# Attention and experts on one core: gate columns from f16 halves of v that the DMA queue turns, one division for two heads, and attention's order by due alone

## The chip, the core and the metric

One core of a Trainium2 chip runs one program. The metric is the device time of that program in microseconds (us). A core has a matrix engine (TensorE, PE in the profile, with its weight loads as PEld), three engines for vectors and scalars (VectorE or DVE, ScalarE or ACT, GpSimd or POOL), a queue that issues transfers (SyncE or SP) and 16 DMA engines that carry them. Each engine works through its own list in order; between engines there are semaphores.

## What is computed

Causal attention with a decay, then a layer of eight experts of which each token uses one. Shapes: 8 batches, 8 heads, 576 tokens, 64 elements a head; 4608 tokens of 512 elements in all.

```python
def _attn_ref(q, k, v, f):
    scores = scale * np.matmul(q, k.transpose(0, 1, 3, 2))
    cum = np.cumsum(np.log(np.clip(f, 0.0001, 1.0)), axis=-1)
    scores = np.where(causal, -1000000000.0, scores + cum[..., :, None] - cum[..., None, :])
    attn = np.exp(scores - np.max(scores, axis=-1, keepdims=True))
    attn = attn / (np.sum(attn, axis=-1, keepdims=True) + 1e-09)
    return np.matmul(attn, v)

def _moe_ref(x, modality_id, w_gate, modality_bias, w1, w2):
    logits = x @ w_gate + modality_bias[modality_id]
    e_idx = np.argmax(logits, axis=1)
    probs = softmax(logits)
    for e in range(E):
        h = np.maximum(x[e_idx == e] @ w1[e], 0.0)
        out[e_idx == e] = probs[e_idx == e, e, None] * (h @ w2[e])
    return out
```

The expert of a token is an argmax over logits, so they are kept close to f32: a value is carried as a high half and a remainder, and a product of two values as three products of halves.

## The kernel before

**Two parts.** Attention comes first; it ends by writing every token's row to a list of its expert (`xs`). Then the experts run in tiles of 256 tokens (class `Moe`). One of its preparations (`early`) lies inside attention.

**Attention's tiles.** The work goes by pairs of heads p (32 of them, four a batch) and by batches b. A pair's steps, with the engine of each: `raw` loads k and q (SP); `hi` and `lo` split them (ScalarE, GpSimd, L372 and L378); `cum` puts the decay sums in place (SP, L383); `mm` computes rough scores for the row maxima (TensorE, L511 to L522) and `mr` reduces them (VectorE); `sp` transposes the maxima (TensorE, L543), `ssp` negates and splits them (VectorE, L549 and L550) and `so` moves them beside q (SP, L557); `s` computes the scores with decay and maximum inside (TensorE, L577 to L592); `e` takes the exponential (ScalarE, L601 and L607); `h` and `r` split it into two f16 parts Ph and Pl (ScalarE L622; GpSimd and VectorE L634); `w`, once a head, forms the weighted sum (TensorE, L660 to L662: 45 matmuls of 128x128 weights, Ph and Pl, by 73 columns); `d`, once a head, divides (VectorE, L671 to L676).

**Gate columns.** The 73 columns of a head's v are a column of ones (the softmax's sum), 64 elements of v, and 8 gate columns: the head's v times its rows of the router's weights. The weighted sum of a gate column is the head's part of the logits, so that the logits come out with attention. v is scaled by a power of two per batch (`vm`, `v1`, `v3`, `v2`: L398 to L428) and split into f16 halves `vh` and `vl` (ScalarE L481, VectorE L488), which have two buffers, for even and odd batches. The gate columns come from a second, transposed f32 copy of v: `vt` loads it for a pair of heads (SP, L457, 320 KB), `gv` scales the router's weights (ScalarE, L453), `kg` multiplies (TensorE, L462: five f32 matmuls with 16 columns, each shown as two records), `kh` and `kl` split the product into the gate columns of vh and vl (ScalarE L467, VectorE L474).

**Routing.** When a batch's heads are divided, `ga` sums the parts of the logits and `rt` picks the expert and the place in its list (VectorE, GpSimd, ScalarE, with a few small matmuls, L723 to L728); `sc` writes the rows out (GpSimd, L769).

**PSUM.** Eight banks: six are three buffers of two banks (`ps`) for `mm` and `s`; one (`po`) holds a weighted sum until it is divided; one (`pb`) is shared by all the small steps: `sp`, `v1`, `v3`, `v2`, `kg` and the router's counts. Only in the last two pairs does the second head's sum use `pb` (function `room`).

**The order.** A planner (class `Plan`) lists all steps with the engine, an estimated duration, what they come after and which buffers they take. `order` is a list scheduler: at each turn it takes the step that could start earliest by a clock of these durations, and the one with the smaller due time where two are equal. The due times are 12.0 us times the pair plus an offset by kind of step from the table `DUE`, with offsets of their own for the first two and last two pairs. The program issues the steps in that order; each engine gets its own in that order.

## Time and profile before

| | us |
|---|---|
| median of 3 runs | 864.05 |
| lowest, highest | 863.62, 870.75 |
| the profiled execution | 868.65 |
| its span, first to last instruction | 866.9 |

The busy share of an engine is an average over two parts with different limits: attention runs until about 384 us, the experts after it. A row of a view of groups has the line of the code, the engine, the operation, what it writes and reads, its shapes and count, then busy us, the mean duration of one in ns, and the idle time of the engine before it. A row of the order of time has start, duration, engine, line, operation, names, shapes and count. Records of TensorE overlap, since matmuls are pipelined: what a block takes is seen from its start to the start of the next.

### The profile page before, as it was taken

To read this page: it belongs to the slowest core of one execution; us is meant where nothing else is said; L and a number is where in the kernel's file an instruction comes from. 1 tells how busy PE (TensorE), PEld (TensorE's weight loads), DVE (VectorE), ACT (ScalarE), POOL (GpSimd) and SP (SyncE) were. 2 spreads that over 40 slices of the span, in tenths; PEclk is the share of its full clock that TensorE was granted. 3 is DMA by queue.
4 is the path that set the end of the run, shared out by engine and by line. 5 is a ranking of instruction groups with operands and counts; after the bars stand their busy time and mean duration, and the time that the engine had idled before them with its cause. 6 is when DMAs were issued, how large, how long until landed. Compare 5 with 4: busy or idle time off the path is not lost. (4 is left out here: it accounts for less than half of the span.)

```text
span 866.9 us, 23516 instructions
## 1 busy us (share of the span) xinstructions
PE 815.1 (94%) x9701; PEld 732.3 (84%) x9701; DVE 649.9 (75%) x1211; ACT 523.0 (60%) x643; POOL 374.7 (43%) x346
## 2 busy tenths in 40 slices
PE   4799999999999999889999999999999999999894
PEld 2689888888888888788899999999999999999673
DVE  7788999999999898868966656666666656666284
ACT  3587777878787878574545544444445435455284
POOL 8476788888888888675610111111100100111110
PEclk9699999999999999999999999999999999999898
DMA  5434344444444442153467611110114311134570
GB/s 192 135 113 140 119 151 135 139 142 134 146 140 153 140 152 99 58 183 124 155 244 276 226 50 49 50 39 35 45 42 146 134 65 49 50 106 166 190 266 29
DMA packets 43301, 108.50 MB, mean 125 GB/s; under 512 B 5423, under 2 KB 5615, under 8 KB 43184
## 3 DMA queue, kind: packets, MB, share of 16 engines
q1 hardware_dynamic: 36480, 85.87, 29.9%
q0 software_dynamic: 6704, 21.02, 6.4%
q8 instruction: 79, 1.29, 0.6%
q14 instruction: 38, 0.31, 0.1%
HBM read 144.19 MB, written 21.80 MB: 191 GB/s over the span
## 5 line engine op out<-in xcount | busy, mean ns | idle before, releaser
L1202 POOL DMA_INDIRECT out_dram<-y,xg x36 | 45.5, 1264 | 344.9 <-DVE y L1201 328.6
L1172 PE MATMUL ph<-xh,w1h 128*128 128x256 f32 x576 | 164.1, 285 | 0.0
L1172 PE MATMUL ph<-xl,w1h 128*128 128x256 f32 x576 | 163.5, 284 | 0.0
L1172 PE MATMUL ph<-xh,w1l 128*128 128x256 f32 x576 | 163.4, 284 | 0.0
L634 POOL TENSOR_TENSOR Pl<-Pt,Ph 128x1024 f16<-128x1024 f32 (+1 forms) x63 | 141.5, 2257 | 7.2 <-ACT Ph L622 6.9
L1118 DVE TENSOR_TENSOR w1l<-raw,w1h 128x1024 fp32r<-128x1024 f32 x78 | 95.9, 1240 | 57.8 <-ACT w1h L1116 57.8
L1116 ACT CAST w1h<-raw 128x1024 fp32r<-128x1024 f32 x80 | 82.7, 1050 | 87.9 <-PE ph L1172 68.3
L1135 ACT CAST w2h<-raw 128x1024 fp32r<-128x1024 f32 x72 | 74.7, 1048 | 98.7 <-issue 57.2
L1136 DVE TENSOR_TENSOR w2l<-raw,w2h 128x1024 fp32r<-128x1024 f32 x72 | 86.8, 1220 | 49.0 <-ACT w2h L1135 47.5
L378 POOL TENSOR_TENSOR X<-raw,X 128x1216 fp32r<-128x1216 f32 x31 | 85.9, 2770 | 63.1 <-ACT X L372 60.0
L1172 PEld LDWEIGHTS ph<-xh,w1h 128*128 128x128 f32 x576 | 111.1, 193 | 1.0 <-DVE hl L1176 0.3
L1172 PEld LDWEIGHTS ph<-xl,w1h 128*128 128x128 f32 x576 | 111.1, 193 | 0.7
L1197 PE MATMUL py<-w2l,hh 128*128 128x512 f32 x288 | 109.5, 390 | 1.7 <-DVE w2l L1136 1.7
L1197 PE MATMUL py<-w2h,hh 128*128 128x512 f32 x288 | 111.1, 395 | 0.0
L1172 PEld LDWEIGHTS ph<-xh,w1l 128*128 128x128 f32 x576 | 111.0, 193 | 0.0
L1197 PE MATMUL py<-w2h,hl 128*128 128x512 f32 x288 | 109.4, 390 | 0.0
L592 PE MATMUL ps<-X 64*128 64x288 f32 (+4 forms) x1152 | 108.2, 318 | 0.0
L660 PE MATMUL po<-vh,Ph 128*128 128x73 f16 x930 | 100.0, 198 | 5.8 <-DVE lgh L676 3.3
L607 ACT ACTIVATE Pt<-ps,lnp 128x576 f32<-128x576 f32 (+1 forms) x96 | 79.6, 864 | 43.0 <-PE ps L592 42.8
L660 PEld LDWEIGHTS <-Ph 128*128 128x128 f16 x960 | 93.7, 98 | 9.9 <-DVE lgh L676 5.0
L662 PE MATMUL po<-vh,Pl 128*128 128x73 f16 x930 | 99.8, 197 | 0.3 <-DVE Pl L634 0.3
L661 PE MATMUL po<-vl,Ph 128*128 128x72 f16 x930 | 99.9, 196 | 0.0
(295 smaller groups left out, 1954.7 us busy)
## 6 DMA issues: line engine op xcount, KB each, us to landing
raw<-in_w_dram SPq DMA_DIRECT2D x84, 1024.0 KB
raw<-in_qk_dram SPq DMA_DIRECT2D x32, 608.0 KB
xg<-xs SPq DMA_DIRECT2D x20, 514.0 KB
vT<-in_vt_dram SPq DMA_DIRECT2D x32, 320.0 KB
vr<-in_v_dram SPq DMA_DIRECT2D x30, 256.0 KB
raw1b<-in_w_dram SPq DMA_DIRECT2D x4, 1024.0 KB
hxg<-xs SPq DMA_DIRECT2D x5, 257.0 KB
vr<-in_v_dram SPq DMA_DIRECT2D x8, 128.0 KB
```

The costliest lines, as they stand in the source:

```text
L378: e.tensor_tensor(X[:, 1], self.get("raw", p), f32(X[:, 0]), ALU.subtract)
L592: nc.tensor.matmul(ps[:, h, c0:c0 + w], X[r, x, k], X[r, y, q], start=False, stop=(j == 2), skip_group_check=True)
L607: nc.scalar.activation(self.get("Pt", (p, i))[:, :, o:o + w], ps[:, :, 0:w], AF.Exp, bias=self.lnp, scale=0.125)
L634: e.tensor_tensor(self.Pl_t[p % 2][:, :, c], self.exps(p, i), self.Ph_t[p % 2][:, :, c], ALU.subtract)
L660: nc.tensor.matmul(o, Ph[:, c0:c0 + P], vh[:, c, hh, :], start=(c == 0), stop=False)
L661: nc.tensor.matmul(o[:, 1:73], Ph[:, c0:c0 + P], vl[:, c, hh, :], start=False, stop=False)
L662: nc.tensor.matmul(o, Pl[:, c0:c0 + P], vh[:, c, hh, :], start=False, stop=(c == ic))
L1116: x = nc.scalar.copy(self.w1h[a], self.raw1[i][a])
L1118: y = e.tensor_tensor(self.w1l[a], self.raw1[i][a], f32(self.w1h[a]), ALU.subtract)
L1136: y = nc.vector.tensor_tensor(self.w2l[a], self.raw2[a], f32(self.w2h[a]), ALU.subtract)
L1172: y = nc.tensor.matmul(ph[:, i, :], w[:, k, f0:f0 + P], x[:, k, :], start=(j == 0), stop=(j == len(m) - 1))
L1197: x = nc.tensor.matmul(py, h[:, k, c * P:c * P + P], w[:, k, :], start=(j == 0), stop=(j == len(m) - 1))
```

## The change

**Gate columns.** For batch 0 all stays (the steps are now named `kg0`, `kh0`, `kl0`). For batches 1 to 7 no transposed copy of v is loaded. When two neighbouring chunks of 128 tokens of vh and vl are split, `tr` issues, for each chunk, two transfers that turn a stretch of 640 f16 columns (all eight heads with their 73 columns each, 584, and what follows them) from 128 tokens by 640 into five blocks of 128 by 128, one for vh and one for vl. `kg` is two steps a batch, of three and two chunks: for each chunk and block three f16 matmuls (high by high, high by low, low by high) with 8 to 24 columns, against a table of the router's weights `wgp` laid out by those columns, scaled by 8192 and split into f16 halves once (`gate_parts`). `kh` and `kl` undo the scale; they cover all heads of their chunks. The rows of vl get a 73rd column (a zero in front), so that both halves have one layout; `setup3` clears what the first turns read.

**One division.** The first head's weighted sum is in `po`, the second's always in `pb`; one division a pair reads both.

**Negated maxima.** The first of the two operations of `ssp` moves from VectorE to ScalarE.

**The order.** The planner has no clock any more: it takes the ready step with the smallest due time whose buffers fit. Due times are 45.49 us times the batch plus an offset by kind of step, by the pair in the batch and by stage (first, second, middle, last batch); there are now fixed orders among the pairs for `mm`, `s` and `w`. The part of `setup2` that the router needs became `setup3`.

The experts are not touched. The diff, cut (`tr`, `w` and `d` stand for the table of offsets):

```diff
-PER = 12.0
+PERIOD = 45.49
 DUE = {
...
+    ('w', 0): ((32.28, 56.39, -7.31, -7.63,), (46.15, 49.38, 59.07, 59.16,), (45.26, 49.41, 55.14, 59.12,), (41.70, 49.59, 105.64, -220.50,),),
+    ('w', 1): ((34.67, 56.24, -7.33, -7.51,), (47.91, 53.73, 60.75, 60.80,), (48.20, 55.23, 60.67, 59.08,), (46.23, 49.33, 113.66, -220.58,),),
+    ('d',): ((24.01, 60.32, 64.95, 69.56,), (19.75, 59.52, 67.40, 69.26,), (41.94, 13.77, 67.55, 69.40,), (19.48, 37.02, 66.21, 317.17,),),
+    ('tr', 1): ((), (10.96,), (3.01,), (-5.62,),), ('tr', 2): ((), (16.32,), (19.43,), (-3.35,),),
...
+        def fits(s):
+            k = [(r, len(taken[r]) - self.bufs[r] + j) for j, (r, _) in enumerate(s["take"])]
+            return all(i < 0 or i < len(taken[r]) and (r, taken[r][i]) in given for r, i in k)
+
...
+            s = st[min((n for n in ready if fits(st[n])), key=lambda n: st[n]["due"])]
+            ready.remove(s["name"])
...
+            given.update(s["free"])
...
-        self.ps_o = pool("a_o", space=PSUM)
-        self.ps_b = pool("a_b", space=PSUM)
+        self.ob = pool("a_o", space=PSUM).tile([P, 2, 512], F32, name="ob")
 
         self.vr = pool("a_vr").tile([P, NJ, 512], F32, name="vr")
         vpool = [pool("a_v0"), pool("a_v1", side="right")]
-        self.vh = [x.tile([P, NJ, NH, 73], F16, name=f"vh{i}") for i, x in enumerate(vpool)]
-        self.vl = [x.tile([P, NJ, NH, 72], F16, name=f"vl{i}") for i, x in enumerate(vpool)]
+        self.rows = [[x.tile([P, VR], F16, name=f"v{n}{i}") for n in "hl"] for i, x in enumerate(vpool)]
+        self.vh, self.vl = ([x[j][:, 0:NJ * VW].rearrange("p (c h e) -> p c h e", c=NJ, h=NH) for x in self.rows] for j in range(2))
...
-        for x in self.vh:
-            nc.gpsimd.memset(x[:, :, :, 0:1], 1.0)
-            nc.gpsimd.memset(x[64:128, 4, :, 0:1], 0.0)
+        for h, l in zip(self.vh, self.vl):
+            nc.gpsimd.memset(h[:, :, :, 0:1], 1.0)
+            nc.gpsimd.memset(h[64:128, 4, :, 0:1], 0.0)
+            nc.gpsimd.memset(l[:, :, :, 0:1], 0.0)
...
+    def setup3(self):
+
+        nc, nb = self.nc, self.nb
+        k = lambda shape, dt, name: self.kp.tile(shape, dt, name=name)
+        for x in self.vh[1], self.vl[1]:
+            nc.gpsimd.memset(x[:, :, :, 65:73], 0.0)
+        for x in self.rows:
+            for y in x:
+                nc.gpsimd.memset(y[:, NJ * VW:], 0.0)
...
-        return self.new(self.ps_b, "pb", key, [P, 512], F32, 1)
+        self.ring["pb"] = [key]
+        self.live["pb", key] = self.ob[:, 1]
+        return self.ob[:, 1]
...
-    def gate_part(self, b):
...
+    def gate_parts(self):
+        nc = self.nc
+        k = lambda shape, dt, name: self.kp.tile(shape, dt, name=name)
+        nc.vector.tensor_scalar(self.wgp, self.wgp, self.sw, GS, ALU.mult, ALU.mult)
+        self.G = [k([P, NJ, 64], F16, f"G{i}") for i in range(2)]
+        nc.scalar.copy(self.G[0], self.wgp)
+        nc.vector.tensor_tensor(self.G[1], self.wgp, self.G[0], ALU.subtract)
+
+    def gate_first(self):
+        self.gv = self.sm.tile([P, 4, 16], F32, name="gv", bufs=1)
+        self.nc.scalar.activation(self.gv, self.wg, AF.Copy, scale=self.get("sv", 0))
+
+    def vt_tile(self, *key):
+        return self.new(self.xp, "vT", key, [P, 2, NJ, P], F16, 3)
...
+    def turn(self, b, c):
+
+        t = self.vt_tile(b, c)
+        for x in range(2):
+            for c2 in range(c, min(c + 2, NJ)):
+                self.owned((("vh", b % 2, c2 // 2), ("vl", b % 2, c2))[x], b)
+            self.nc.sync.dma_start_transpose(out=t[:, x], in_=self.rows[b % 2][x][:, VW * c:VW * c + NJ * P])
+
+    GC = [(0, 3), (3, 5)]
+
+    def key_gate(self, b, i):
+        pg, first = self.bank(("kg", b, i)), True
+        for c in range(*self.GC[i]):
+            t = self.get("vT", (b, c))
+            for k, (e0, e1) in enumerate(((0, 16), (8, 32), (24, 48), (40, 56), (56, 64))):
+                for x, y in ((0, 0), (0, 1), (1, 0)):
+                    self.nc.tensor.matmul(pg[:, 64 * c + e0:64 * c + e1], t[:, x, k], self.G[y][:, k, e0:e1],
+                                          start=first, stop=True, skip_group_check=True)
+                    first = False
+
+    def key_gate_hi(self, b, i):
+        c = slice(*self.GC[i])
+        pg = self.get("pb", ("kg", b, i))[:, 0:64 * NJ].rearrange("p (c h e) -> p c h e", h=NH, e=8)
+        self.own(("gh", b % 2, i), b)
+        self.nc.scalar.activation(self.vh[b % 2][:, c, :, 65:73], pg[:, c], AF.Copy, scale=1.0 / GS)
+
+    def key_gate_lo(self, b, i):
+        c = slice(*self.GC[i])
+        pg = self.get("pb", ("kg", b, i))[:, 0:64 * NJ].rearrange("p (c h e) -> p c h e", h=NH, e=8)
+        self.owned(("gh", b % 2, i), b)
+        self.own(("gl", b % 2, i), b)
+        self.nc.vector.scalar_tensor_tensor(self.vl[b % 2][:, c, :, 65:73], pg[:, c], 1.0 / GS, self.vh[b % 2][:, c, :, 65:73],
+                                            ALU.mult, ALU.subtract)
...
-        nc.vector.tensor_scalar(mT[:, 0], pt, -1.0, None, ALU.mult)
+        nc.scalar.activation(mT[:, 0], pt, AF.Copy, scale=-1.0)
...
-        name, key = self.room(u)
-        po = self.bank(key) if name == "pb" else self.new(self.ps_o, "po", u, [P, 512], F32, 1)
+        po = self.bank(("w", u)) if h else self.ob[:, 0]
+        self.own(("w", h), u)
         for ic in range(NJ):
             o = po[:, ic * 73:ic * 73 + 73]
             for c in range(ic + 1):
                 c0 = OFF[c] + (ic - c) * P
                 nc.tensor.matmul(o, Ph[:, c0:c0 + P], vh[:, c, hh, :], start=(c == 0), stop=False)
-                nc.tensor.matmul(o[:, 1:73], Ph[:, c0:c0 + P], vl[:, c, hh, :], start=False, stop=False)
+                nc.tensor.matmul(o, Ph[:, c0:c0 + P], vl[:, c, hh, :], start=False, stop=False)
                 nc.tensor.matmul(o, Pl[:, c0:c0 + P], vh[:, c, hh, :], start=False, stop=(c == ic))
 
-    def divide(self, u):
+    def divide(self, p):
         nc, sm = self.nc, self.sm
-        b, hh = divmod(u, NH)
+        b, hp = divmod(p, 4)
+        for h in range(2):
+            self.owned(("w", h), 2 * p + h)
         x = self.once(self.xp, "x", b, [P, NJ, 514], F32, 2)
-        self.own(("x", b % 2, hh), b)
-        o4 = self.get(*self.room(u))[:, 0:NJ * 73].rearrange("p (c e) -> p c e", e=73)
-        z = sm.tile([P, NJ, 1], F32, name="z")
-        first = nc.vector.tensor_scalar(z, o4[:, :, 0:1], PSC * 1e-9, self.get("sv", b), ALU.add, ALU.mult)
+        self.own(("x", b % 2, hp), b)
+        self.get("pb", ("w", 2 * p + 1))
+        o4 = self.ob[:, :, 0:NJ * 73].rearrange("p h (c e) -> p h c e", e=73)
+        z = sm.tile([P, 2, NJ, 1], F32, name="z")
+        first = nc.vector.tensor_scalar(z, o4[:, :, :, 0:1], PSC * 1e-9, self.get("sv", b), ALU.add, ALU.mult)
         nc.vector.reciprocal(z, z)
-        nc.vector.tensor_tensor(x[:, :, hh * D:hh * D + D], o4[:, :, 1:65], z.broadcast_to([P, NJ, D]), ALU.mult)
+        to = x[:, :, 2 * hp * D:2 * hp * D + 2 * D].rearrange("p c (h d) -> p h c d", h=2)
+        nc.vector.tensor_tensor(to, o4[:, :, :, 1:65], z.broadcast_to([P, 2, NJ, D]), ALU.mult)
 
         self.owned(("bias", b % 2), b)
-        x = nc.vector.tensor_tensor(self.get("lgh", b)[:, :, :, hh], o4[:, :, 65:73], z.broadcast_to([P, NJ, 8]), ALU.mult)
-        self.divided = self.divided[-2:] + [(first, x.ins.name)]
-        self.own(("lgh", b % 2, hh), b)
+        to = self.get("lgh", b)[:, :, :, 2 * hp:2 * hp + 2].rearrange("p c e h -> p h c e")
+        last = nc.vector.tensor_tensor(to, o4[:, :, :, 65:73], z.broadcast_to([P, 2, NJ, 8]), ALU.mult)
+        self.divided = self.divided[-1:] + [(first, last.ins.name)]
+        self.own(("lgh", b % 2, hp), b)
...
+            add("ssp", k, [("ACT", 0.22), ("DVE", 0.27)], 0, self.shift_split, k, [("sp", p), prev("so", 2)], free=[("pb", ("t", p))])
...
+                add("w", (u,), "PE", 1.5, self.weighted, (u,), [("w", u - 2) if p else None] + [("r", p, i) for i in range(3)] + [("vl", b, c) for c in range(NJ)] + ([("kl", b, i) for i in range(2)] if b else [("kl0", p % 4)]), take=("pb", ("w", u)) if h else ("po", p))
+            add("d", k, "DVE", 1.45, self.divide, k,
+                [("w", 2 * p), ("w", 2 * p + 1), ("gb", b)] + ([("sc", b - 2, c) for c in range(NJ)] if b > 1 else []), free=[("po", p), ("pb", ("w", 2 * p + 1))])
...
+                add("gv", (), "ACT", 0.25, self.gate_first, (), [("gs",), ("v2", b)])
+                for hp in range(4):
+                    add("vt", (hp,), "SP", 0.4, self.load_vt, (hp,), [("kg0", hp - 3) if hp > 2 else None, ("vt", hp - 1) if hp else None], lands=328e3)
+                    add("kg0", (hp,), "PE", 1.1, self.key_gate_0, (hp,), [("vt", hp), ("gv",)], take=("pb", ("kg", 0, hp)))
+                    add("kh0", (hp,), "ACT", 0.135, self.key_gate_hi_0, (hp,), [("kg0", hp), ("setup2",)])
+                    add("kl0", (hp,), "DVE", 0.15, self.key_gate_lo_0, (hp,), [("kh0", hp)], free=[("pb", ("kg", 0, hp))])
+            for c in range(NJ if b else 0):
+                two = range(c, min(c + 2, NJ))
+                add("tr", k + (c,), "SP", 0.8, self.turn, (b, c), [("vl", b, x) for x in two] + [("vh", b, x // 2) for x in two] +
+                    [("tr",) + divmod(NJ * b + c - 1, NJ) if b > 1 or c else ("vt", 3), ("setup3",),
+                     ("kg", b, 0) if c > 2 else ("kg", b - 1, min(c, 1)) if b > 1 else ("kg0", c + 1)], lands=480e3)
+            for i in range(2 if b else 0):
+                add("kg", k + (i,), "PE", (1.1, 0.75)[i], self.key_gate, (b, i), [("tr", b, c) for c in range(*self.GC[i])] + [("gp",)], take=("pb", ("kg", b, i)))
+                add("kh", k + (i,), "ACT", (0.24, 0.18)[i], self.key_gate_hi, (b, i), [("kg", b, i)])
+                add("kl", k + (i,), "DVE", (0.27, 0.2)[i], self.key_gate_lo, (b, i), [("kh", b, i)], free=[("pb", ("kg", b, i))])
...
+    wgp = np.zeros((NJ * P, NH, 8), moe_w_gate.dtype)
+    for h in range(NH):
+        wgp[73 * h + 1:73 * h + 1 + D, h] = moe_w_gate[D * h:D * h + D]
```

236 lines of the change are left out of this document (89 added, 147 removed), and 78 rows, old and new, of the table DUE.

## The prediction

> **What bounds the kernel now.** I read the page first, then the view by stretches (first with the borders of attention, then three equal ones in its middle), then the order of TensorE's work inside one batch, then groups, issues and waits.
>
> ```profile
> span 866.9 us, 23516 instructions
> ```
>
> Columns of the next view: length, then busy us (and instructions) of PE, PEld, DVE, ACT and POOL, granted clock, share of the DMA engines, GB/s.
>
> ```profile
> 0.00:356.00 356.00, 326.83 (x6250) 290.96 (x6251) 318.23 (x753) 265.53 (x324) 277.05 (x258) 0.98 0.42 136
> 356.00:384.00 28.00, 22.41 (x455) 19.92 (x452) 17.53 (x59) 18.08 (x22) 18.16 (x21) 0.94 0.45 156
> 384.00:867.00 483.00, 465.89 (x3008) 421.42 (x3004) 314.12 (x401) 239.40 (x299) 79.51 (x68) 0.98 0.33 115
> ```
>
> Everything that the change edits runs before 384 us. The 483 us of experts behind it have the same instructions afterwards; they only start earlier or later. So the whole question is the length of attention.
>
> ```profile
> 104.00:148.00 44.00, 42.10 (x841) 37.73 (x838) 40.66 (x98) 34.38 (x43) 36.07 (x31) 1.00 0.44 144
> 148.00:192.00 44.00, 42.37 (x846) 37.98 (x846) 40.66 (x96) 34.38 (x43) 36.11 (x31) 1.00 0.44 144
> 192.00:236.00 44.00, 42.12 (x845) 37.98 (x845) 40.66 (x98) 34.40 (x43) 36.09 (x31) 1.00 0.44 144
> ```
>
> The middle repeats itself, batch after batch. TensorE is busy 42.1 to 42.4 us of 44 (96%) at full clock, VectorE 40.66 (92%), GpSimd 36.1 (82%), ScalarE 34.4 (78%), and the DMA engines carry 0.44 of what they could. TensorE is the bound, VectorE is close behind it, and some 1.8 us of each batch are TensorE's idle time. The exact period stands in TensorE's order: the same step (the transpose of the maxima of v) in two batches.
>
> ```profile
> 190.39 0.28 PE L406 MATMUL pb<-ident,am 128*3 128x128 f32 x1
> ...
> 192.26 0.21 PE L660 MATMUL po<-vh,Ph 128*128 128x73 f16 x1 [0.26 <-DVE a L415]
> ...
> 193.87 0.38 PE L421 MATMUL pb<-a,ones 1*128 1x1 f32 x2
> ...
> 194.81 0.26 PE L577 MATMUL ps<-later,id 64*128 64x128 bf16 x4
> ...
> 195.51 1.29 PE L462 MATMUL pb<-gv,vT 128*128 128x16 f32 x10
> 196.73 0.29 PE L511 MATMUL ps<-after,id 64*128 64x64 bf16 x6
> ```
> ```profile
> 234.73 0.27 PE L406 MATMUL pb<-ident,am 128*3 128x128 f32 x1
> ```
>
> 234.73 - 190.39 = 44.34 us a batch, four pairs of heads at 11.1 us.
>
> **Part 1, gate columns on TensorE (the term that carries the forecast).** One key gate of before is the five f32 matmuls of a pair, ten records at L462: it starts at 195.51 and the next work at 196.73, so it holds TensorE for 1.22 us, or 4.88 us for a batch's four. Batch 0 keeps this path; batches 1 to 7 lose 28 x 1.22 = 34.2 us. In their place come 75 f16 matmuls a batch (five chunks, five blocks of rows, three products), 525 in all, with 128x128 weights and 8 to 24 moving columns. Two rows bound the price of one. The running counts of the router have f16 weights of the same size and 8 to 32 columns:
>
> ```profile
> 227.01 0.24 PE L728 MATMUL pb<-roh,ones 128*128 128x32 f16 x4
> 227.11 0.19 PE L660 MATMUL po<-vh,Ph 128*128 128x73 f16 x1
> ```
>
> Four of them pass in 0.10 us, 25 ns each. The weighted sums, 45 matmuls with 73 columns, go from 192.26 to 193.87: 1.61 us, 36 ns each. I take 25 ns, since weights and columns are nearly the same: 525 x 0.025 = 13.1 us; the dearer end is 18.8. Net -34.2 + 13.1 = **-21.1 us**, bounds -15.4 and -21.1. The low part's 73rd column (L661) adds one column in 72 to 840 matmuls of 33 ns: +0.4 us.
>
> **Part 2, VectorE and ScalarE.** Rows of the view of groups between 96 and 336 us (busy us, mean ns of one):
>
> ```profile
> L673 DVE TENSOR_TENSOR x<-po,z 128x320 f32<-128x320 f32 x44 | 21.6, 491 | 1.7
> L676 DVE TENSOR_TENSOR lgh<-po,z 128x40 f32<-128x40 f32 x43 | 9.5, 222 | 0.0
> L671 DVE TENSOR_SCALAR z<-po,sv 128x5 f32<-128x5 f32 x44 | 9.3, 212 | 0.8
> L672 DVE RECIPROCAL z<-z 128x5 f32<-128x5 f32 x44 | 8.4, 191 | 1.5
> ...
> L549 DVE TENSOR_SCALAR mT<-pb 10x128 bf16<-10x128 f32 x22 | 5.9, 269 | 2.7 <-PE pb L543 2.7
> L467 ACT ACTIVATE vh<-pb 128x80 f16<-128x80 f32 x21 | 5.2, 249 | 3.5 <-PE pb L462 3.5
> L474 DVE TENSOR_TENSOR vl<-pb,vh 128x80 f16<-128x80 f32 x21 | 4.8, 229 | 0.0
> ...
> L453 ACT ACTIVATE gv<-wg,sv 128x64 f32<-128x64 f32 x6 | 2.1, 348 | 6.1 <-DVE sv L428 6.1
> ```
>
> A division is 491 + 222 + 212 + 191 = 1116 ns now, 2232 a pair. From 40 to 320 elements the price rises by 269 ns, 0.96 ns an element; so 640 elements cost about 798, 80 elements 260, and with the two short ones one division for both heads is 1.46 us. VectorE saves 0.77 us a pair, 3.1 a batch. The negated maxima go to ScalarE: -1.08 a batch. Four gate remainders of 229 ns become two of 192 and 128 elements, by the same slope 337 and 275: -0.3. Together -4.5, so VectorE falls from 40.66 to about 36.2 us a batch. ScalarE gets four copies at about 0.25, loses `gv` (0.35) and turns four `kh` of 249 ns into two of about 0.36 and 0.30: +0.3, to 34.7. None of this lies on the bound by itself, so I count it 0. Its cover is TensorE's new need of about 39.3 us a batch; its worth is that VectorE doesn't become the bound. Without it VectorE's 40.66 would stand above 39.3 and eat 1.4 us of the 3 saved in each batch.
>
> **Part 3, the turns on the DMA queue.** The 28 loads of 320 KB go, nine MB in all. Each later batch issues ten turning transfers of 160 KB (128 x 640 f16) from SP instead.
>
> ```profile
> L457 SPq DMA_DIRECT2D vT<-in_vt_dram x32: 327/334/1165, 11.8 to 336.4; - x32
> ```
> ```profile
> L383 SPq DMA_DIRECT2D Sk<-chl x32: 642/684/819, 9.7 to 342.7; - x32
> ```
> ```profile
> SPq L383 <- PE pb L543: 79.9, 17, 6.5
> SPq L383 <- PE ps L592: 26.7, 5, 5.4
> ```
>
> No row shows a turn. Below, it costs what a load costs: 0.334 us to issue, and 160 KB at the full rate that 144 GB/s at a share of 0.44 stands for (327 GB/s), 0.50 us. Above, by the row with the most issue time for its bytes (L383, 0.684 us for 6.8 KB), 16 us. I take the lower end, as shape (128 partitions, one tile) is that of the loads: 3.3 us of SP and 5.0 us of DMA a batch, against 1.3 and 4.0 removed. SP has room: it stood 107 us of the 240 in the two waits above alone. Behind a turn that waits for the last `vl`, the raw loads, `cum` and the shift's `so` are queued in order, and the scores wait for `so`. The chain of the gate columns gets longer (v, its scale, both halves, turn, gate, halves, weighted sum), but the halves of v have two buffers, so it has a batch's length, 41 us, to hide in. Hence 0; the cover is gone where ten turns take longer than a batch.
>
> One page of the Trainium skill speaks for this and one against. Advanced Engine Details and Errata, section X-Bar Transpose (TRN2), has such transfers as fast as plain ones, 350 to 400 GB/s; by that the sum is unchanged. VectorE: DVE Perf Modes, section The three transpose paths, gives 1309 ns for one 128x128 block; fifty blocks a batch, one after another, would be 65 us, and the kernel about 1010 us. No run here shows which holds.
>
> **Part 4, order and banks.** The even weighted sum stays in its bank, the odd one goes into the bank of all the small steps (`pb`), and one division frees both. `pb` was held by each key gate from 195.51 to the end of its remainder:
>
> ```profile
> 198.79 0.23 DVE L474 TENSOR_TENSOR vl<-pb,vh 128x80 f16<-128x80 f32 x1
> ```
>
> 3.5 us, four times a batch. Now each pair holds it for the odd sum (1.61), a hand-over of about 0.25 and the division (1.46): 3.3 us, four times, and two gates besides. So `pb` is fuller by about 4 us of 41. The new order lists by due alone. Its effect is bounded by TensorE's idle time: all of it gone is -1.9 us in each of seven batches, -13; as much again added is +13. I take 0. At the start the second gate table is loaded and split: its 160 KB are 0.5 us of DMA, and two VectorE operations of 320 elements (491 ns) stand in
>
> ```profile
> 20.00:24.00 4.00, 2.10 (x27) 1.24 (x26) 3.96 (x8) 1.21 (x1) 2.17 (x1) 1.00 0.49 168
> 24.00:28.00 4.00, 2.35 (x16) 1.71 (x16) 3.12 (x10) 0.74 (x1) 0.59 (x1) 0.53 0.46 156
> ```
>
> where VectorE is full and TensorE is not: +1 at most, 0 if put later. GpSimd's added clearing is covered by its idle time from 24 us on (0.59 of 4 us busy).
>
> **Sum.** -21.1 + 0.4 = **-20.7 us**. The profiled execution took 868.65 us (span 866.9), so it would take 848. It lay above the median of the runs, 864.05; from that the forecast is **843 us**. A measurement of this kernel tells about 1% (8.6 us) from no change.
>
> **Rivals.**
> A, *the order also closes idle time*: half of 1.9 us in seven batches (6.6) and the 5.6 us that TensorE stands still between 356 and 384 us: 831 us. For it: the divisions on which the weighted sums wait are halved. Against: the middle is already at 96%. 0.20.
> B, *another engine or the loop through the buffers becomes the bound and half the gain stays*: 854 us. For it: GpSimd's 36.1 and VectorE's 36.2 us of 41.3 are 87% each, with waits on one another. 0.15.
> C, *the gain is hidden*, as the idle time grows by what the gates gave back: 862 us. Against: with TensorE busy 42.2 us of 44, only 1.8 us are left in which another limit can have ruled. 0.07.
> D, slower, *the shift waits for `pb`*. The shift's transpose needs `pb`; in before its result was sent off at 189.56 + 1.12 = 190.68 and the scores began at 194.81 (L577):
>
> ```profile
> 189.56 1.12 SPq L557 DMA_DIRECT2D Sq<-mT  x2
> ```
>
> The transfer has 4.1 us for that. No row shows its flight, so the slack lies between 0 and 4.1 us; I take the middle, 2.1. A transpose behind a full 3.3 us of `pb` would show 1.2 us a pair: 28 x 1.2 = +34, net 877 us. It loses from 0.74 us a pair on. Against: the order can place the transpose before the odd sum. 0.06.
> E, *turns slower than a batch*: 4.4 us each is where ten fill the old period; at the far end of 16 us they take 160 us a batch and the kernel some 1670 us. 0.04. That the change doesn't do what it says gets no chance of its own, since load and matmuls of before are replaced outright.
>
> **How the numbers follow.** The forecast has 0.48; its own range is 836 to 850 (dearer matmuls 849, half of the middle's idle time gone 837). Rivals A, B and C reach down to 828 and up to 862; D and E, 0.10, and the tails of A stay outside. Faster by over 1% (under 855.4): the forecast, A and 0.13 of B, 0.81. Within 1%: the rest of B and C, 0.09. Slower: D and E, 0.10.
>
> **What would show it.** Right: a batch's period near 41.3 us, TensorE still near 96%; the new gate's 45 and 30 matmuls in about 1.1 and 0.75 us; VectorE near 36 us a batch; a division near 1.46 us. Wrong: TensorE's idle time above 3 us a batch with the shift or `pb` as releaser (D), or with the turns landing late in front of the gates (E); SP waiting on a turn while `so` is due; a period at 44 with TensorE under 92% (C).

## The result, and the profile after

The changed kernel takes 911.27 us (median of 4 runs, 910.34 to 915.60) against 865.38 us for the kernel before in the same sessions: a ratio of 1.053, 95% interval 1.047 to 1.059. It is slower by 46 us; the forecast was 843 us. Its profiled execution took 910.34 us.

Below, attention ends where the experts' first matmul with their weights starts; the last batch's router is still at work then. The view by stretches (columns as in the prediction) with that border, before and after:

```profile
0.00:386.50 386.50, 351.74 (x6773) 313.38 (x6774) 338.26 (x816) 286.12 (x347) 297.55 (x280) 0.98 0.42 137
386.50:867.00 480.50, 463.39 (x2934) 418.92 (x2930) 311.62 (x396) 236.90 (x297) 77.17 (x67) 0.98 0.33 116
```
```profile
0.00:422.60 422.60, 364.01 (x7020) 316.01 (x7020) 322.65 (x646) 287.94 (x359) 294.45 (x287) 0.92 0.53 131
422.60:909.00 486.40, 464.09 (x2932) 419.90 (x2928) 310.10 (x393) 236.40 (x296) 75.21 (x68) 0.98 0.33 114
```

Attention is 36.1 us longer, and there the mean granted clock is 0.92 and not 0.98. The experts take 6 us more with the same instructions; over the kernels below with the same routing they took 477 to 484 us, and the changed kernel's 486 lies just above that, so these 6 are not read as an effect of the change. The start of the router's counts marks the end of each batch's middle; read from the trace (after: L774, before: L723), in us:

| | before | after |
|---|---|---|
| counts of batch 0 | 94.0 | 90.0 |
| batch 0 to 5 | 221.7 | 243.9 |
| batch 5 to 6 (early tables of the experts) | 47.5 | 61.6 |
| batch 6 to 7 | 33.5 | 36.7 |
| attention ends | 386.5 | 422.6 |

So 22.2 us are lost in five batches of the middle, and 14.1 in the one interval with the early tables. The start is 4 us earlier, and 3 more are lost behind. Two batches of the middle and that interval, after:

```profile
190.50:238.20 47.70, 43.90 (x882) 38.19 (x882) 38.82 (x76) 34.57 (x44) 35.85 (x30) 0.93 0.61 140
238.20:286.20 48.00, 43.96 (x881) 38.20 (x881) 38.79 (x75) 34.68 (x44) 35.86 (x30) 0.93 0.56 138
...
333.90:395.50 61.60, 47.49 (x911) 40.71 (x911) 45.04 (x103) 36.91 (x46) 36.17 (x33) 0.88 0.39 98
```

The period is 47.8 us where 41.3 was forecast. TensorE is busier than before, though it has less to do; in the same rows the clock is 0.93. The border of a batch shows where both come from (time line after; start, us, engine, line):

```profile
234.93 2.77 POOL L385 TENSOR_TENSOR X<-raw,X 128x1216 fp32r<-128x1216 f32 x1 [1.64 <-ACT X L379]
...
235.40 2.36 DVE L763 TENSOR_TENSOR roh<-iota_e,rei 128x40 f32<-128x40 f32 x1
...
237.95 0.18 DVE L766 TENSOR_TENSOR roh<-roh,valid 128x40 f16<-128x40 f32 x1
...
238.19 0.18 PE L774 MATMUL ob<-roh,tri 128*128 128x40 f16 x1 [1.51 <-DVE roh L766]
```

The one-hot comparison, 40 elements, starts at 235.40, while GpSimd works on an SBUF tile from 234.93 to 237.70, and it ends 0.06 us after that. The counts wait for it, TensorE stands 1.51 us in front of them, and everything behind them in its order stands too. The same seconds in steps of 3.4 us:

```profile
234.10:237.50 3.40, 2.29 (x38) 1.96 (x35) 3.37 (x4) 3.37 (x5) 2.57 (x1) 1.00 0.55 117
237.50:240.90 3.40, 2.29 (x44) 1.91 (x43) 3.37 (x10) 0.95 (x2) 2.54 (x4) 1.00 0.16 35
240.90:244.30 3.40, 2.46 (x56) 1.85 (x56) 2.64 (x7) 2.92 (x4) 1.83 (x6) 1.00 0.22 24
244.30:247.70 3.40, 3.40 (x38) 2.50 (x36) 2.97 (x7) 2.47 (x4) 2.90 (x2) 0.51 0.64 241
247.70:251.10 3.40, 3.40 (x46) 2.81 (x42) 2.67 (x7) 1.78 (x2) 3.24 (x4) 0.50 0.62 185
```

Three steps with TensorE busy 67 to 72%, then two at half the clock: 6.8 us in which it does 3.4 us of work, in each of these batches. The period grew by 3.5 us, which is as much; whether the half clock is the cause is for the runs below.

### The profile page after: what moved, and what is told of

Read it like the earlier page. It is cut to its first block, busy times and chain, and to the rows that moved or that the text cites. A ratio compares the mean times of both kernels' runs of the same rounds, so it can differ in the third digit from the quotient of the medians.

```text
span 908.6 us, 23981 instructions
## 1 busy us (share of the span) xinstructions
PE 828.1 (91%) x9946; PEld 735.9 (81%) x9946; DVE 632.7 (70%) x1039; ACT 524.3 (58%) x655; POOL 369.7 (41%) x354
## 5 line engine op out<-in xcount | busy, mean ns | idle before, releaser
L684 POOL TENSOR_TENSOR Pl<-Pt,Ph 128x1024 f16<-128x1024 f32 (+1 forms) x63 | 142.1, 2266 | 39.3 <-ACT Ph L672 39.1
L1189 ACT CAST w2h<-raw 128x1024 fp32r<-128x1024 f32 x72 | 74.7, 1048 | 96.2 <-issue 58.7
L1190 DVE TENSOR_TENSOR w2l<-raw,w2h 128x1024 fp32r<-128x1024 f32 x72 | 86.9, 1221 | 49.0 <-ACT w2h L1189 47.5
L706 PE MATMUL ob<-vh,Ph 128*128 128x73 f16 x960 | 109.0, 202 | 12.1 <-DVE mT L600 9.0
L642 PE MATMUL ps<-X 64*128 64x288 f32 (+4 forms) x1152 | 114.6, 324 | 0.0
L707 PE MATMUL ob<-vl,Ph 128*128 128x73 f16 x960 | 108.8, 202 | 0.0
L708 PE MATMUL ob<-vh,Pl 128*128 128x73 f16 x960 | 108.4, 202 | 0.0
L707 PEld LDWEIGHTS <-Ph 128*128 128x128 f16 x960 | 97.0, 101 | 12.9 <-issue 12.7
L706 PEld LDWEIGHTS <-Ph 128*128 128x128 f16 x960 | 96.6, 101 | 6.3 <-issue 4.9
```

The lines of the kernel that those rows point to most:

```text
L642: nc.tensor.matmul(ps[:, h, c0:c0 + w], X[r, x, k], X[r, y, q], start=False, stop=(j == 2), skip_group_check=True)
L684: e.tensor_tensor(self.Pl_t[p % 2][:, :, c], self.exps(p, i), self.Ph_t[p % 2][:, :, c], ALU.subtract)
L706: nc.tensor.matmul(o, Ph[:, c0:c0 + P], vh[:, c, hh, :], start=(c == 0), stop=False)
L707: nc.tensor.matmul(o, Ph[:, c0:c0 + P], vl[:, c, hh, :], start=False, stop=False)
L708: nc.tensor.matmul(o, Pl[:, c0:c0 + P], vh[:, c, hh, :], start=False, stop=(c == ic))
L1189: x = nc.scalar.copy(self.w2h[a], self.raw2[a])
```

## The experiments

The theory after reading the trace, T1: the operations are a gain; the new order lets the router's counts stand in front of ready work, VectorE's comparison is held by GpSimd, and the pause costs the clock besides. Rivals: T2, the new gate path (turns, longer chain); T3, the odd sum in the shared bank and the one division. Each kernel was compared with runs of the kernel before on the same chip; its ratio to them is given with the 95% interval. Where the experiment changes a table of due times, the diff shows the entry.

**Counts later in the order.**
```
-    ('rt', 4): ((74.76,), (77.82,), (77.53,), (30.28,),),
+    ('rt', 4): ((76.76,), (79.82,), (79.53,), (30.28,),),
```


> Order only: the due time of the router's counts is raised by 2 us for the batches 0 to 6, so that TensorE is given mm(1), scores (2) and the router product of the next pair ahead of the counts. Nothing is computed otherwise. T1 (the order: TensorE stands idle 1.5 to 1.7 us in front of the counts in every batch, waiting for VectorE's one-hot comparison, and pays a half clock for 6.8 us behind it): the gap in front of the counts is gone, the granted clock in the middle goes from 0.93 to 1.0, the period from 47.7 to 43 to 44.5 us, the time to 885 to 895 us (the last two batches are left as they are). T2 (the new gate path with its turns is what is late): the period stays at 47.7 and the time at 908 to 914 us. T3 (one odd sum and one division hold the weighted sums): the period stays as well.

926.71 us, ratio 1.072 (1.065 to 1.080): slower than the changed kernel, a miss for T1 as put. The pause went to the next reader of VectorE (waits of TensorE from 90 to 351 us: in total, times, longest):

```profile
PE ps L627 <- DVE mt L582: 19.9, 5, 4.0
```

The scores wait for maxima that stand in VectorE's queue behind the same comparison and the product after it, which is now long as well (2.38 and 2.09 us at 239 to 244 us). What is late is VectorE, and not TensorE's order of the counts.

**One-hot table in PSUM.**
```
+        nc.vector.tensor_copy(self.ob[:, 0, 384:424], self.iota_e.rearrange("p c e -> p (c e)"))
-            nc.vector.tensor_tensor(oh, self.iota_e, ei.broadcast_to(s3), ALU.is_equal)
+            nc.vector.tensor_tensor(oh, self.ob[:, 0, 384:424].rearrange("p (c e) -> p c e", e=8), ei.broadcast_to(s3), ALU.is_equal)
```


> The order is kept; VectorE's one-hot comparison reads its table of expert numbers from PSUM and not from SBUF, so that it may run beside GpSimd's work. Everything is computed as before. T1 with the shared SBUF port as the cause of the late comparison: the comparison falls from 2.36 us to under 0.5 us, the 1.5 us gap in front of the counts goes to under 0.3 us, the granted clock in the middle to 1.0, the period to 43 to 44.5 us, the time to 880 to 892 us. T1 without the port (the comparison is late since its inputs are): the comparison is shorter, but the gap stays over 1 us, 905 to 914 us. T2 and T3: 908 to 914 us.

904.82 us (the median of three runs; a fourth took 915.92), ratio 1.042 (1.032 to 1.051). The comparison fell to 199 ns, but the product behind it rose (groups from 90 to 334 us, the changed kernel first):

```profile
L763 DVE TENSOR_TENSOR roh<-iota_e,rei 128x40 f32<-128x40 f32 x5 | 12.2, 2449 | 0.2
...
L766 DVE TENSOR_TENSOR roh<-roh,valid 128x40 f16<-128x40 f32 x5 | 0.9, 183 | 0.0
```

```profile
L767 DVE TENSOR_TENSOR roh<-roh,valid 128x40 f16<-128x40 f32 x6 | 8.7, 1451 | 0.0
...
L764 DVE TENSOR_TENSOR roh<-ob,rei 128x40 f32<-128x40 f32 x6 | 1.2, 199 | 2.2 <-ACT vh L517 1.6
```

The hold moved on to the next operation with two SBUF operands. That same product had taken 183 ns in the changed kernel, where it starts as GpSimd's operation ends: it is not long by itself. Two of four batches in the middle ran at the full clock, with a period of 44.6 us:

```profile
196.40:244.20 47.80, 44.23 (x883) 38.28 (x883) 37.92 (x76) 34.33 (x44) 35.94 (x30) 0.93 0.59 141
244.20:288.80 44.60, 41.20 (x881) 35.78 (x881) 37.38 (x76) 34.80 (x44) 38.14 (x30) 1.00 0.57 146
```

**Filler in the pause.**
```
+            for _ in range(30):
+                nc.tensor.matmul(self.ob[:, 0, 384:512], self.tri, self.ones, start=True, stop=True)
```


> The order is kept; in front of the router's counts of each batch TensorE does 30 products of 128x128 by 128 columns in f16 into a spare part of a PSUM bank (work that nobody reads, about 1.6 us at the full clock), in the pause where it waits for the one-hot matrix. T1: the pause itself stays lost, but TensorE is never idle for long, so that the half clock of 6.8 us after it is gone: 3.4 us for each of 6 batches and some in the tail, the time 885 to 895 us, granted clock 1.0 in the middle. If the half clock has nothing to do with the pause, the time stays at 908 to 914 us. T2: 908 to 914 us.

907.06 us, ratio 1.049 (1.042 to 1.055). The clock recovered by half (mean 0.96 in the middle, one half-clock window a batch and not two), but the filler stands itself behind a wait (7.6 us over five batches, now with the gates' lower halves as releaser), and its 1.7 us of work stand in front of the counts, about as much as one half-clock window costs. The period stayed at 47.8. Inconclusive on the price of the clock.

**Plain copies for turns.**
```
-            self.nc.sync.dma_start_transpose(out=t[:, x], in_=self.rows[b % 2][x][:, VW * c:VW * c + NJ * P])
+            self.nc.sync.dma_start(t[:, x].rearrange("p k t -> p (k t)"), self.rows[b % 2][x][:, VW * c:VW * c + NJ * P])
```


> The turns by DMA are replaced by plain copies of the same bytes between the same two SBUF tiles, so that the gate columns of batches 1 to 7 are wrong and with them the routing; the end of the attention is compared (first product of the experts: 422.6 us with the turns, 386.5 us before the change), not the time. T2 (the turns are slow, hold SP's queue for 1.24 us each, or load the DMA engines): the end of the attention falls to 385 to 400 us and the period to 43 to 45 us. T1: the turns are hidden, period 47.7 us and end of the attention 418 to 424 us, though SP's issue of one falls below 1.24 us.

Attention ends at 422.2 us (422.6 with turns); one batch:

```profile
189.90:237.50 47.60, 43.85 (x882) 38.14 (x882) 38.77 (x76) 34.60 (x44) 35.84 (x30) 0.93 0.43 140
```
 The issue of one on SyncE fell by more than half (views by line, turns of the changed kernel and the copies; ns min/median/max):

```profile
L498 SPq DMA_TRANSPOSE vT<-vh x35: 1206/1238/2614, 66.4 to 382.3; - x35
```
```profile
L498 SPq DMA_DIRECT2D vT<-vh x35: 465/537/1410, 63.0 to 379.5; - x35
```

T2 falls as far as the turns go: they are hidden, although each costs SyncE 1.24 us.

**Less for TensorE in the kernel before.** The test of the step on which the forecast rested.
```
-        for c in range(NJ):
-            self.nc.tensor.matmul(pg[:, 16 * c:16 * c + 16], t[:, P * c:P * c + P], g[:, hp], start=True, stop=True)
+        for c, n in ((0, 3), (3, 2)):
+            self.nc.tensor.matmul(pg[:, 16 * c:16 * (c + n)].rearrange("p (n e) -> p n e", n=n), t[:, P * c:P * c + P],
+                                  g[:, hp:hp + 1].broadcast_to([P, n, 16]), start=True, stop=True)
```


> The kernel before, in its own order, with TensorE's part of the key gates cut: 2 f32 products of 48 and 32 columns for each pair of heads in place of 5 of 16, so that the gate columns (and the routing) are not the reference's; everything else is issued as before. This takes about 2.7 us of TensorE's work out of each batch (4.83 us to about 2.1), as much as the change takes out, and moves nothing. The period of a batch and the end of the attention are compared (44.34 us and 386.5 us before), not the time alone. F1 (the step on which the forecast rested: TensorE sets the period, and freed time comes off): period 41.4 to 42 us, attention ends at 364 to 370 us. F2 (the chain through VectorE and GpSimd sets the period, and freed time of TensorE turns into waits): period 43.8 to 44.4 us, TensorE idle 4 to 5 us in a batch and not 1.9.

```profile
178.50:222.40 43.90, 39.95 (x822) 35.58 (x822) 41.22 (x98) 34.45 (x43) 36.35 (x31) 1.00 0.45 144
```

TensorE does 39.95 us a batch and not 42.4, and the period is 43.96 and not 44.34; attention ends at 380.1. Of 2.5 us, 0.4 came off: F2. TensorE had been busy 96% in the kernel before, and in that order its work was not the bound.

**The gate path alone taken back, in the changed order.** The turns become f32 loads, the two gate steps the f32 products of batch 0; the scaled weights are made in front of the first.
```
+        if i == 0:
+            self.nc.scalar.activation(self.new(self.sm, "gw", b, [P, 4, 16], F32, 2), self.wg, AF.Copy, scale=self.get("sv", b))
```


> The changed kernel in its own order with the gate path alone taken back: the columns of batches 1 to 7 come again from f32 loads of the turned v and f32 products (20 a batch, 10 in each of the two steps), on the same places of the order, in the same bank, with no turns by DMA. F1 (the order is worse, but TensorE's freed 2.7 us a batch are a gain in it): 11 to 20 us slower than the changed kernel, 922 to 931 us. F2 (TensorE's freed time is lost in waits that the order makes): within 6 us of the changed kernel, 905 to 917 us. T2 (the turns are the loss): faster than the changed kernel by over 10 us.

932.25 us, ratio 1.079 (1.075 to 1.084), 21 us above the changed kernel. But the scaling on ScalarE brought a wait of its own in front of the gates (1.44 us a batch), so this doesn't price the gates; a later run does.

**Both tables in PSUM.** As the second run, and the valid rows too.
```
+        nc.vector.tensor_copy(self.ob[:, 0, 424:429], self.valid)
-            nc.vector.tensor_tensor(oh16, self.get("roh", b), self.valid.rearrange("p (c o) -> p c o", o=1).broadcast_to(s3),
+            nc.vector.tensor_tensor(oh16, self.get("roh", b), self.ob[:, 0, 424:429].rearrange("p (c o) -> p c o", o=1).broadcast_to(s3),
```


> As the run with the one-hot table in PSUM, and the table of valid rows is read from PSUM too, so that both of VectorE's small products ahead of the counts (one-hot, and one-hot by valid, which took 1.31 to 1.38 us in that run) may run beside GpSimd. T1 (VectorE held by GpSimd in the router's chain, and the half clock that follows TensorE's pause): the granted clock is 1.0 in all of the batches 2 to 5, the period 44 to 44.7 us in each of them (there it was 47.8, 47.8, 44.6, 44.7), the time 885 to 897 us. If the half clock hangs on other gaps: some batches stay at 47.7, 900 to 910 us.

884.51 us, ratio 1.025 (1.020 to 1.029) where the changed kernel has 1.053: by the ratios some 25 of the 46 us are gone. In the profiled executions attention ends at 404.4 us and not 422.6: the two small products of VectorE, with what follows from them, cost 18.2 us. The rest is the experts' part (477.0 and 486.0), which isn't put down to the edit. Batches 2 to 5 (the first three rows) and the interval with the early tables:

```profile
183.60:227.60 44.00, 40.98 (x884) 35.67 (x883) 36.35 (x76) 34.93 (x44) 38.17 (x31) 1.00 0.63 152
227.60:270.40 42.80, 40.77 (x884) 35.64 (x883) 36.34 (x76) 34.73 (x44) 38.09 (x31) 1.00 0.72 156
270.40:314.60 44.20, 42.19 (x884) 36.85 (x883) 36.71 (x76) 34.75 (x44) 39.19 (x31) 0.96 0.59 150
314.60:377.60 63.00, 50.37 (x915) 43.70 (x914) 43.35 (x101) 38.98 (x48) 36.72 (x34) 0.83 0.41 98
```

The period is 43.67 us. The clock is 1.00 in two of these three batches and 0.96 in the third, where 1.00 was expected in all. T1 holds in its second half: VectorE is late behind GpSimd, and the clock falls behind the pause. The loss that is left sits in the last interval, 63.0 us against 47.5.

**Order of the last batch.** 171 due times of the last batch and of the early tables set anew by prices from the traces.


> Order only, and only of the last batch and of the early tables of the experts: their due times are set anew, the batches 0 to 6 keep theirs. In the changed kernel the interval between the router's counts of the batches 5 and 6 is 61.6 us against 47.7 in the middle (before: 47.5 against 44.3): SyncE waits for the tables with the last pair's sums behind it in its queue, and TensorE pauses four times for 1.2 to 2.5 us. If that is the order: the interval falls to 52 to 56 us and the time by 5 to 10 us, to 900 to 907 us. If it is the change's operations (the turns of the last batch, 1.5 us each on SyncE's queue): within 3 us of 911 us.

907.93 us, ratio 1.052 (1.047 to 1.057), against 1.053: no difference, and the interval is 62.8. A miss. It tells little of the operations, since only one new order was tried.

**Both tables in PSUM, in the kernel before.** The same two lines; to hold the tables, the bank of the weighted sum becomes one fixed tile.


> The kernel before, in its own order, with the same two tables (expert numbers, valid rows) read from PSUM as in the run that brought the changed kernel to 884.5 us. If the shared SBUF port was a price of the change's order alone: 858 to 866 us, period 44.3 us, no difference that counts. If the two tables are a gain for any order: 850 us or less.

860.71 us, ratio 0.994 (0.991 to 0.998). Both products fell there too, before (first fence) and with the tables in PSUM:

```profile
L712 DVE TENSOR_TENSOR roh<-iota_e,rei 128x40 f32<-128x40 f32 x5 | 7.9, 1589 | 0.2
L715 DVE TENSOR_TENSOR roh<-roh,valid 128x40 f16<-128x40 f32 x6 | 3.2, 540 | 0.0
```
```profile
L721 DVE TENSOR_TENSOR roh<-roh,ob 128x40 f16<-128x40 f32 x6 | 1.1, 185 | 0.0
L718 DVE TENSOR_TENSOR roh<-ob,rei 128x40 f32<-128x40 f32 x5 | 1.0, 200 | 0.2
```

The period fell from 44.34 to 43.40 us. The kernel before paid the same hold; it did not pay the clock for it.

**Gate path back, both tables in PSUM** (the sixth run's edit on the seventh's).


> The changed kernel with both tables in PSUM (884.5 us, period 43.67) and the gate path alone taken back to f32 loads and f32 products in the same places of the order, so that the gates are priced where the clock stays up. F1 (TensorE's freed time counts): 2.7 us of work a batch come back as time, period 46 to 47 us, 900 to 910 us. F2 (it is lost in waits, as the run of the kernel before with short gates showed: 0.4 us of 2.7): period 43.9 to 44.6, 884 to 892 us.

945.77 us, ratio 1.093 (1.085 to 1.102). The wait for the scaled weights was there again:

```profile
PE ob L510 <- ACT gw L505: 4.3, 3, 1.4
```

**The last pair's sums first.** In the changed kernel SyncE's queue in the late interval is (time line after):

```profile
379.96 2.27 SPq L498 DMA_TRANSPOSE vT<-vl  x1
382.32 1.24 SPq L498 DMA_TRANSPOSE vT<-vh  x1
383.61 1.27 SPq L498 DMA_TRANSPOSE vT<-vl  x1
387.61 1.22 SPq L1143 DMA_DIRECT2D xg<-xs  x2
388.92 0.74 SPq L390 DMA_DIRECT2D Sk<-chl  x1
```
```profile
392.29 0.61 PE L567 MATMUL ps<-Sk,Cq 64*128 64x192 bf16 x4 [2.35 <-DMA Sk<-chl]
```
The experts' loads wait until VectorE has made their table, and the sums `chl` wait behind them.
```
-    ('cum',): (..., (-27.35, -51.38, -30.97, 28.88,),),
+    ('cum',): (..., (-27.35, -51.38, -30.97, -20.00,),),
```


> The changed kernel with both tables in PSUM, and the last pair's sums are put on SyncE's queue ahead of the last batch's turns and of the early tables' loads (one due time, 28.88 to -20.00); nothing else. In that kernel TensorE stood 3.51 us for these sums at 374 us, at the end of five windows of half clock. If the queue of SyncE is the tail's loss: 4 to 8 us faster, 876 to 881 us. If VectorE's 5.5 us of early tables set the same pause a little later: within 2 us of 884.5 us.

893.95 us, ratio 1.034 (1.028 to 1.041). The interval fell as expected, from 63.0 to 58.7, and attention still ended later, at 406.6 and not 404.4: the middle, whose order is the same, took 229.2 us from batch 0 to 5 and not 222.9, with half-clock windows in other batches. The experts' part was 6 us longer as well (483.4 and 477.0). So two kernels with the same order in the middle differ by 6 us there, and a few us between such kernels can't be put down to their edit.

**All due times searched anew**, with both tables in PSUM, by a model with prices from the traces.


> The changed kernel's operations with both tables in PSUM, and all due times searched anew with the turns (2.5 us of SyncE a pair of tiles), the port and the early tables priced as the traces have them; by those prices the period is 43.4 us, the interval at the early tables 48 and not 56 us. If the loss is the order and the prices that it was made with: 862 to 876 us, interval of the router's counts from batch 5 to 6 under 53 us (63.0 with the change's order). If the operations themselves cost it: over 880 us.

944.58 us, ratio 1.092 (1.085 to 1.099). TensorE's waits from 97 to 373 us:

```profile
PE ob L746 <- DVE mT L640: 20.9, 9, 2.7
PE ob L548 <- DVE roh L803: 15.9, 4, 4.1
```

The odd sum (L746) waits for the shared bank until the shift's halves are taken out of it. The gates (L548) start when VectorE's one-hot comparison ends, which reads its table from the tile that they write; whether the table's new place makes that wait isn't shown. The time lies where it was expected if the operations themselves cost it. But these waits are hardly there in the changed kernel, so this run shows a bad order and settles nothing about the operations.

**The negation on ScalarE alone, in the kernel before.**
```
-        nc.vector.tensor_scalar(mT[:, 0], pt, -1.0, None, ALU.mult)
+        nc.scalar.activation(mT[:, 0], pt, AF.Copy, scale=-1.0)
```


> The kernel before in its own order, with one part of the change alone: the negated shift's upper half is made by ScalarE and not by VectorE. If the negation is harmless (my forecast: 0): 860 to 867 us. If ScalarE's queue holds the shared bank longer (one of the rivals): TensorE waits for mT 1 to 2 us more at each pair, some 30 to 60 us in all, 890 us or more.

861.55 us, ratio 0.998 (0.996 to 1.000). Harmless.

**The negation back on VectorE, in the changed kernel with both tables in PSUM.**


> The changed kernel with both tables in PSUM (884.5 us) and the negation given back to VectorE, on the same place of the order. If ScalarE's queue is the wait at the shared bank in the tail (2.62 us at 338 us, and the half clock after it): the interval of the router's counts from batch 5 to 6 falls from 63.0 to under 58 us, the time to 872 to 880 us. If VectorE is as late at that place: within 4 us of 884.5 us.

884.09 us, ratio 1.022 (1.017 to 1.028): no difference. The late interval fell here too, to 58.6, and the middle took 226.5 us; so neither this edit nor the sums put first can be credited with the 4 us.

**The gate path back without the extra wait**: the weights scaled with v's upper halves.


> As the undone gate path with both tables in PSUM (945.8 us), but the scaled gate weights are made ahead of time (with the upper halves of v), so that TensorE doesn't stand 1.44 us in front of the gates for them. F1 (gates are worth TensorE's time): period 46 to 47 us, 900 to 910 us. F2 (lost in waits): period 43.9 to 44.6 us, 884 to 892 us. If it stays over 930 us, it is the half clock that f32 gates bring in this order, not their own time.

909.54 us, ratio 1.053 (1.048 to 1.058), against 1.025 with the new gates.

```profile
193.30:241.40 48.10, 47.16 (x849) 41.92 (x848) 37.06 (x78) 35.13 (x46) 35.91 (x30) 0.89 0.42 132
```

So in this order the new gates are worth some 24 us. TensorE is idle under 1 us of 48 here. The period is 4.0 us longer than with the new gates, and the gates' own work only 2.8 (4.83 against 2.05); part of the rest is clock (0.89).

**The one division alone, in the kernel before.** The odd sum goes into the shared bank, one division frees both; each step at its time of the order before, the even head first.
```
-        po = self.bank(key) if name == "pb" else self.new(self.ps_o, "po", u, [P, 512], F32, 1)
+        po = self.bank(("w", u)) if h else self.ob[:, 0]
```


> The kernel before with one part of the change alone: the odd head's sum in the bank that all small products share, and one division for both heads, every step at its time of the order before (within a pair the even head first). If the shared bank is harmless (my forecast: 0 to -3 us): 858 to 868 us. If the odd sum holds the bank that shift, gates and counts need (the rival in which the shift waits): TensorE waits 1 to 2 us a pair, period over 48 us, 900 us or more.

976.56 us, ratio 1.130 (1.123 to 1.137), period 61.35 us.

```profile
224.80:286.10 61.30, 50.93 (x848) 44.70 (x846) 38.35 (x82) 34.62 (x43) 35.71 (x30) 0.86 0.32 103
```
```profile
PE ob L1800 <- DVE lgh L2014: 9.8, 6, 1.6
PE ob L1759 <- DVE lgh L2014: 8.2, 5, 1.6
PE ob L1800 <- DVE mT L1888: 7.5, 11, 0.7
```

Gates (L1800) and the scale of v (L1759) wait for the end of the division (L2014) or for the shift (L1888), all at that bank. T3 is right about the bank: in the old order this part can't be had.

**Short gates with both tables in PSUM, in the kernel before.**


> The kernel before in its own order with both tables in PSUM (period 43.40 us, attention ends at 381.0) and with the short gates of the earlier run (2 products for 5, so that the gate columns and the routing are not the reference's): 2.7 us less of TensorE's work a batch. The end of the attention and the period are compared. If TensorE bounds that kernel: period 40.7 to 41.3 us, attention ends at 360 to 364 us. If the chain through VectorE still does: period 42.6 to 43.4 us, TensorE idle 3 us or more a batch, attention ends at 375 to 381 us.

```profile
175.60:218.20 42.60, 39.79 (x824) 35.76 (x822) 39.84 (x98) 34.45 (x43) 36.27 (x31) 1.00 0.47 148
```

Period 42.65 (43.40 without the short gates), attention ends at 374.4 (381.0). Of 2.3 us of TensorE 0.75 came off: still not its bound.

**The two harmless parts together, in the kernel before.**


> The kernel before in its own order with both tables in PSUM and the negation on ScalarE, everything computed as before. If the two gains add: ratio 0.990 to 0.994, 856 to 859 us. If the negation is nothing: 0.994, 860 us. If VectorE's lighter queue only moves the waits: 0.996 or more.

861.05 us, ratio 0.996 (0.994 to 0.999). The gains don't add. VectorE's work fell from 39.9 to 38.6 us a batch, and the period stayed (43.40 and 43.56 us). So shortening either of the two fullest engines alone hardly moves this kernel. The lowest ratio of this study is that of the kernel before with both tables in PSUM, 0.994 and 860.71 us; the intervals of this run and that one overlap.

## Why the prediction was wrong

The step that failed is the effect of the order, "bounded by TensorE's idle time: all of it gone is -1.9 us in each of seven batches, -13; as much again added is +13. I take 0". Idle time did grow by about as much (1.9 to 3.8 us a batch), but the bound had left out the clock, and behind the pause the clock halved for 6.8 us in each batch. A second step failed beside it: that a batch gets shorter by what TensorE no longer has to do.

- **The bound.** "TensorE is the bound" was read off 96% busy. Both runs with short gates refute it for the old order: 2.3 to 2.5 us less gave 0.4 and 0.75. That is rival C, the gain hidden. Against it I had argued that only 1.8 us are left for another limit; the same two runs show that another limit had ruled all the same. What sets the period is not shown; a chain through several engines could leave each of them nearly full. In the changed kernel with the clock repaired the period is 43.67 us, not 41.3, though taking the gates back costs 24 us there. So something else in the changed kernel's middle costs about what the gates give; the runs don't separate it. At the full clock TensorE was busy 40.8 to 41.0 us a batch, not 39.3, though the gates were nearly as short as forecast; this isn't explained.
- **Part 1** was priced right as work of TensorE. The second of a batch's two new gate steps, 30 products:

```profile
243.35 0.90 PE L508 MATMUL ob<-G,vT 128*128 128x16 f16 x30 [0.56 <-DVE a L422]
```
0.90 us with the pipeline's end; both steps hold TensorE for 2.1 us a batch against 4.83 (forecast 1.9 against 4.88). As time the term exists in the new order (24 us when it is taken back) and hardly in the old one.
- **Part 2.** One division is 226 + 216 + 825 + 298 ns = 1.57 us; forecast 1.46 (rows from 90 to 334 us):

```profile
L723 DVE TENSOR_TENSOR x<-ob,z 128x640 f32<-128x640 f32 x20 | 16.5, 825 | 0.8
...
L727 DVE TENSOR_TENSOR lgh<-ob,z 128x80 f32<-128x80 f32 x20 | 6.0, 298 | 0.0
L720 DVE TENSOR_SCALAR z<-ob,sv 128x10 f32<-128x10 f32 x20 | 4.5, 226 | 15.0 <-PE ob L708 8.4 <-PE ps L642 4.2 <-PE ps L572 2.4
L721 DVE RECIPROCAL z<-z 128x10 f32<-128x10 f32 x20 | 4.3, 216 | 0.7
```
The negation at 0 was right. VectorE came to 38.8 and not 36.2 us a batch; the division explains 0.4 of it and the comparison with its product 0.5 (2.45 and 0.18 us, before 1.59 and 0.54), the rest isn't traced.
- **Part 3.** A turn costs SyncE 1.24 us to issue, nearly four times the 0.334 of a load that I had taken. The size was wrong; the cover named there held, and the cost of 0 with it: plain copies in place of turns leave the period at 47.6 us (47.8), and over one batch the share of the DMA engines was 0.61 with turns and 0.43 with copies. The Trainium skill, VectorE: DVE Perf Modes, section The three transpose paths, gives 1309 ns for one block; the prediction's estimate from it, 65 us a batch with the blocks one after another, does not hold here. The Trainium skill, Advanced Engine Details and Errata, section X-Bar Transpose (TRN2), has turns as fast as plain transfers; in this trace they took more of the DMA engines' time than copies, and were hidden.
- **Part 4.** "`pb` is fuller by about 4 us of 41" was counted as nothing. Alone in the old order it costs 17 us a batch, the clock that it loses (0.86) among them. Rival D had a wait at this bank at 0.06 and +1.2 us a pair, with the shift waiting for the odd sum; in the changed kernel the order avoids most of it in the middle, and at the end one odd sum stands 2.6 us for the shift.
- **Why VectorE was late.** The Trainium skill, SBUF — State Buffer, section SBUF: two separate sides, says that a VectorE operation with two SBUF inputs and a GpSimd operation that reads SBUF lock each other out for a whole instruction. The trace agrees: 2.36 us ending with GpSimd's, 0.20 with one input in PSUM. The row (1589 ns for 40 elements) stood in a view of before that I had read ahead of the forecast, and I passed over it.

The account, of the 36.1 us by which attention is longer: 18.2 are the two held products and the clock behind them, shown by moving their tables to PSUM. Of the 17.9 that are left, the late interval has 15.5 (63.0 against 47.5) and the one behind it 2.9; the middle is even with that of before, where 21 us of gain were forecast. In the late interval TensorE waits for VectorE behind the early tables, for SyncE's queue and for the shared bank, and the clock is 0.83; their shares weren't told apart. One part of it is a third held operation, a cast of eight elements in the early tables (changed kernel; then the same cast before):

```profile
382.09 2.39 POOL L684 TENSOR_TENSOR Pl<-Pt,Ph 128x1152 f16<-128x1152 f32 x1 [2.42 <-ACT Ph L672]
382.22 2.32 DVE L1039 CAST c_nta<-c_nia 1x8 f32<-1x8 int32 x1
```
```profile
354.03 0.23 DVE L985 CAST c_nta<-c_nia 1x8 f32<-1x8 int32 x1
```

It ends 0.06 us after GpSimd's operation, and it still takes 2.30 us with both tables in PSUM. The maxima, remainders and the rest of VectorE's queue stand behind it, and TensorE waits 2.49 us at 388.76 for a remainder (L684) that is queued there. Before, an operation next to it took 1.10 us (L982), so not all of this is new. No run moves it; what it is worth is not shown. Whether another order of the changed operations would beat the kernel before stays open; the ones that were tried do not.

## What to carry to other kernels

An engine that is busy 96% isn't shown to be the bound: shorten its work in the old kernel and see whether the period follows (here 0.4 us of 2.5). An order made on a planner's prices is only as good as the dearest price that it has wrong; look for operations of a few elements that take microseconds, since those are waits in disguise. Where a change lengthens pauses of TensorE, price the clock behind them, and count who else uses a buffer that is given a second, longer job.
